# Sending every thirteenth load in two parts, partitions 0-119 and 120-127, in a two-layer decode step with its gradients

## The chip, the cores and the metric

The kernel runs on one core of one Trainium2 chip. The metric is the device time of one execution in microseconds (us); lower is better. Below, PE is TensorE, DVE is VectorE, ACT is ScalarE, POOL is GpSimd, SP is the engine from which most transfers are issued. "Line L257" is a line of the kernel before. MiB are 2^20 bytes, MB are 10^6.

## The reference: what is computed

Two identical blocks, attention against a long cache and a small MLP, are applied one after the other to a batch of two single tokens, and then the gradients of all inputs and weights are taken:

```python
def _A_ref(x, k_cache, v_cache, wq, wo):          # x 2x1x1024, caches 2x4x16384x128
    q = (x @ wq).reshape(B, Sq, 32, 128).transpose(0, 2, 1, 3)
    k = jnp.repeat(k_cache, 8, axis=1)
    v = jnp.repeat(v_cache, 8, axis=1)
    p = _softmax(jnp.einsum("bhqd,bhkd->bhqk", q, k) * 128 ** -0.5)
    o = jnp.einsum("bhqk,bhkd->bhqd", p, v)
    return o.transpose(0, 2, 1, 3).reshape(B, Sq, 4096) @ wo
def _B_ref(x, w1, b1, w2, b2):                    # w1 1024x3584, w2 3584x1024
    h = _gelu(_layernorm(x) @ w1 + b1)
    return h @ w2 + b2
for _ in range(2):
    x = x + _A_ref(_layernorm(x), k_cache, v_cache, wq, wo)
    x = x + _B_ref(_layernorm(x), w1, b1, w2, b2)
# outputs: x, and the gradients of x, k_cache, v_cache, wq, wo, w1, b1, w2, b2
```

All arrays are bf16. The two caches are 32 MiB each and are used by both layers, forward and backward, so they are read several times; their gradients, 32 MiB each, are most of what is written.

## The kernel before: tiles, queues and order of the work

The caches are cut into eight groups (batch times key head) of 128 partitions, and each group into four chunks of 32 rows a partition. A chunk is a tile of 128 partitions by 4096 bf16, 1 MiB, that is 8192 contiguous bytes for each partition. Weights come in tiles of the same size, or 896 KiB for w1: one row of 8192 or 7168 bytes a partition, or four rows of 2048 bytes.

All bulk loads are issued from SP's queue, in the order in which the program calls for them:

- `w_load` (L254, issue at L257) for the weights that pass through once (`w_pass`, L288, and the class `Ahead`, L343);
- `kv_load` (L404, issue at L409) for chunks of K and V in `attn_fwd` (L501) and `attn_bwd` (L593); a few chunks go to tiles that are kept (`keepK`, `keepV`, `keepxK`, `keepxV`);
- `load` in `wq_steps` (L877, issue at L886) for pieces of wq;
- `load_next` (L1198, issues at L1204 for wq and L1207 for K and V) in the last stage.

The loads share a pool `ld` of `NLD` = 7 buffers (L75, L81): SP's queue waits at a load until the last reader of the tile that was in the buffer is done. The work runs in stages: layer 0 forward and layer 1 forward (each a pass over wq, then K and V group by group, then wo and w1; w2 follows in layer 0), then layer 1 backward (w1, wo, V and K again, wq, w2), the MLP of layer 0 backward, and last the attention of layer 0 backward. `attn_fwd` turns each K chunk on TensorE (L420, copied out at L153 by ACT and L156 by DVE), takes scores (L573), exponentials (L537), and accumulates the V products (L452).

The last stage, from about 700 us, is where the outputs are made and stored. Its loop (L1434) turns a chunk of V (L1450), takes scores (L1312), and makes the gradients of K and V (`kv_pair`, L1247, matmuls at L1258) and of the weights (`dw_units`, L1162, matmuls at L1175). DVE (L164) and ACT (L161) cast the products into tiles, and `store` (L1137) sends these out. Stores go through POOL's software queue until L1480, where `pace["queue"]` becomes SP's queue for the last twelve. In this stage the pool's buffers are handed round by hand: `load_next` takes a tile whose store was issued or whose readers are done, so that a load may wait for a store to land. `pump` (L1209) issues loads ahead as far as free tiles allow. L1538 is the end of the program, where SP waits for the last stores.

Waits between engines are semaphores that the framework places from the program's reads and writes: a reader of a tile waits for every transfer that wrote it.

Of the kernel before, what the change touches and what calls it, by code (L numbers as in the profile page):

```python
# [2 lines left out]

# [20 lines left out]
def kernel(  # L24
# [24 lines left out]
    nc = tc.nc  # L49
# [4 lines left out]
    B, _, D = A_x.shape  # L54
# [11 lines left out]
    TC = 32  # L66
# [23 lines left out]
    ps_x = ctx.enter_context(tc.tile_pool(name="ps_x", bufs=4, space=PSUM))  # L90
    ps_acc = ctx.enter_context(tc.tile_pool(name="ps_acc", bufs=1, space=PSUM))
    ps_sm = ctx.enter_context(tc.tile_pool(name="ps_sm", bufs=1, space=PSUM))

    def pt(shape, dtype, name):
        return ps_tp.tile(shape, dtype, name=name, tag="tp")
# [74 lines left out]
    def wide_in(x2):  # L170

        return x2.unsqueeze(1).to_broadcast([128, WIDE // 2, 2])

    def wide_out(ps, c0):

        return ps[:, c0:c0 + WIDE].rearrange("p (a b) -> p a b", b=2)
# [77 lines left out]
    def w_load(W, j0, rb, n_cols):  # L254
        wt = ld.tile([128, LDW], BF16, name="wt", tag="ld")
        wv = wt[:, 0:rb * n_cols].rearrange("p (j n) -> p j n", j=rb)
        nc.sync.dma_start(wv, W[j0 * 128:(j0 + rb) * 128, :].rearrange("(j p) n -> p j n", p=128))  # L257
        return wv

    class BwdPipe:  # L260
# [57 lines left out]
    def turn(view, new_tp):  # L318

        tp = new_tp()  # L320
        for o in range(8):
            PE.transpose(tp[:, o, :], view[:, o * 128:(o + 1) * 128], ident[:])  # L322
        evac_bf16(view, tp[:].rearrange("p a b -> p (a b)"), 1024)
# [80 lines left out]
    def kv_load(w, g, c):  # L404
        keep = w + str(c) if g == G - 1 else w if (g, c) == (XG, 0) else None
        t = held_tiles[keep] if keep else ld.tile([128, LDW], BF16, name="kv_" + w, tag="ld")
        if keep not in held:
            src = Kv if w == "K" else Vv
            nc.sync.dma_start(t[:].rearrange("p (t d) -> p t d", d=128), src[g, :, c * TC:(c + 1) * TC, :])  # L409
            if keep:  # L410
                held.add(keep)
        return t[:].rearrange("p (t d) -> p t d", d=128)
# [12 lines left out]
    class Acc:  # L425
# [16 lines left out]
        def quad(self, c, q, coef=None):  # L442
            coef = coef or self.coef
            if q == 0 and self.get is not None:
                self.cv = self.get(c)
            elif q == 0:
                self.cv = self.pre.pop(c) if c in self.pre else kv_load(self.src, self.g, c)
            for i in range(8):
                u = c * CP + q * 8 + i
                cg = 32 * (i % 4)  # L450
                t = 2 * (q * 8 + i)
                PE.matmul(self.acc[cg:cg + 16, :], lhsT=coef(u),  # L452
                          rhs=self.cv[:, t:t + 2, :].rearrange("p t d -> p (t d)"),
                          start=False, stop=True, tile_position=(0, cg), skip_group_check=True)
# [46 lines left out]
    def attn_fwd(l, q_bf, rbc, oT, groups):  # L501
# [79 lines left out]
        while s < len(slots) + 2 or sch.busy():  # L581
            sch.s = s
            if s < len(slots):
                g, c, b = slots[s]
                if b == 0:
                    cv = kv_load("K", g, c)
                kTs[s] = emit_T(cv, b, True)
            sch.run_slot(1 if s < len(slots) else 2)
            if 2 <= s < len(slots) + 2:
                score(s - 2)  # L590
            s += 1

    def attn_bwd(l, do_bf, dqT, dn, groups, ahead):  # L593
# [40 lines left out]
        def post(g, c):  # L634
# [21 lines left out]
            if g == groups[-1]:  # L656
                accs[g].pre[c] = kv_load("K", g, c)
                if c == NCH - 1:
                    for k in range(NLD - 2):
                        ahead.load(k)  # L660
                        j0, rb = ahead.chunks[k]
                        w2_q.extend(lambda j=j: ahead.row(j) for j in range(j0, j0 + rb))
# [212 lines left out]
    wq_v = A_wq.rearrange("(j p) n -> p j n", p=128)  # L875

    def wq_steps(l, kv, dqT, dn, new_tp, new_ps, get_=None, done_=lambda *job: None):  # L877

        hs = slice(kv * 8, kv * 8 + 8)
        box = {}  # L880

        def load(j):
            wt = ld.tile([128, LDW], BF16, name="wqt", tag="ld") if get_ is None else get_("wq", kv, j)
            box[j] = wt[:].rearrange("p (j n) -> p j n", j=4)
            if get_ is None:
                nc.sync.dma_start(box[j], wq_v[:, j:j + 4, kv * D:(kv + 1) * D])  # L886

        def turn_row(j):
            turn(box[j - j % 4][:, j % 4, :], new_tp)

        def products(j0=0):
            ps = new_ps()
            for j in range(j0, DJ):
                for o in range(8):
                    PE.matmul(wide_out(ps, 2 * j), lhsT=box[j - j % 4][:, j % 4, o * 128:(o + 1) * 128],
                              rhs=wide_in(dq_all[:, kv * 8 + o, 2 * l:2 * l + 2]), start=(o == 0), stop=(o == 7))
            V.tensor_tensor(out=dn[:, j0:DJ], in0=dn[:, j0:DJ],
                            in1=ps[:, 2 * j0:2 * DJ].rearrange("p (j b) -> p j b", b=2), op=ALU.add)
            for j in (0, 4):
                done_("wq", kv, j)  # L900

        def dq_in():
            for b in range(2):
                V.tensor_copy(out=dq_all[:, hs, 2 * l + b], in_=dqT[:, b * HKV + kv, :])

        return [lambda j=j: load(j) for j in (0, 4)], dq_in, [lambda j=j: turn_row(j) for j in range(DJ)], products, box
# [31 lines left out]
    for k in range(NLD - 2, len(w2b.chunks)):  # L938
        w2b.load(k)
        j0, rb = w2b.chunks[k]  # L940
# [193 lines left out]
    def load_tile():  # L1134
        return (by_read or by_store if opening["on"] else by_store or by_read).popleft()

    def store(out_ap, view, tile_):  # L1137
        pace["queue"].dma_start(out_ap, view)
        if tile_ is not None:
            by_store.append(tile_)  # L1140

# [10 lines left out]
    def dbias(rows, i, n, out_ap, name):  # L1152
        p = 32 * i
        row = new_home()
        for c0 in range(0, n, 512):
            ps = mx()
            PE.matmul(ps[p:p + 1, :], lhsT=ones_bf[p:p + 4, 0:1], rhs=rows[p:p + 4, c0:c0 + 512], start=True, stop=True,
                      tile_position=(p, p))
            evac_cast(row[p:p + 1, c0:c0 + 512], ps[p:p + 1, :], 512)
        store(out_ap.rearrange("(o f) -> o f", o=1), row[p:p + 1, 0:n], row)  # L1160
# [37 lines left out]
    def load_next():  # L1198
        job = jobs.popleft()
        t = loaded[job] = load_tile()  # L1200
        open_loads.append(job)
        if job[0] == "wq":
            src = wq_v[:, job[2]:job[2] + 4, job[1] * D:(job[1] + 1) * D]
            nc.sync.dma_start(t[:].rearrange("p (j n) -> p j n", j=4), src)  # L1204
        else:
            src = (Kv if job[0] == "K" else Vv)[job[1], :, job[2] * TC:(job[2] + 1) * TC, :]
            nc.sync.dma_start(t[:].rearrange("p (t d) -> p t d", d=128), src)  # L1207

    def pump(most, spare):  # L1209
        while jobs and len(open_loads) < most and n_free() > spare:  # L1210
            load_next()

    def get(*job):
        while job not in loaded:
            load_next()
        return loaded[job]
# [30 lines left out]
    def kv_pair(w, i, h):  # L1247

        g, c = chunks[i]
        if h == 0:  # L1250
            stgs[w, i] = new_home()
        sv_ = stgs[w, i][:].rearrange("p (b r t d) -> p b r t d", r=4, t=2, d=128)
        blk, Qm = blks[w, i], qms[w, g]
        o = 0 if w == "V" else NB
        pss = [mx() for _ in range(4)]
        for b in range(2):
            for r in range(4):
                PE.matmul(pss[r][:, b * 256:(b + 1) * 256], lhsT=blk[32 * r:32 * r + 32, o + 2 * h + b, :],  # L1258
                          rhs=Qm[32 * r:32 * r + 32, :, :].rearrange("p a b -> p (a b)"), start=True, stop=True,
                          tile_position=(32 * r, 0))  # L1260
        for r in range(4):
            evac_cast(sv_[:, 2 * h:2 * h + 2, r], pss[r][:].rearrange("p (b t d) -> p b t d", b=2, t=2), 512)
        if h == 0:
            split[w, i] = pace["short"] or i >= NC - 2
        if h == 1 or split[w, i]:
            lo = h if split[w, i] else 0
            dst = (dVv if w == "V" else dKv)[g, :, c * TC + lo * TC // 2:c * TC + (h + 1) * TC // 2, :]
            store(dst, stgs[w, i][:, lo * LDW // 2:(h + 1) * LDW // 2].rearrange("p (t d) -> p t d", d=128),
                  stgs[w, i] if h == 1 else None)
# [214 lines left out]
    i, g = NC - 1, order[-1]  # L1484
    kv = g % HKV
# [57 lines left out]
```

## Time and profile before

| what | value |
|---|---|
| median of 3 runs | 1139.71 us (1137.65 to 1144.74) |
| the profiled execution, its own time | 1138.65 us |
| its span in the profile | 1136.9 us, 40053 instructions |
| busy: PE, PEld (weight loads), DVE, ACT, POOL | 944.5, 730.9, 633.7, 564.7, 70.9 us |
| mean granted TensorE clock | 0.857 of full speed |
| moved by DMA | 449.31 MB in 91983 packets, mean 395 GB/s |
| read from and written to the main memory | 348.14 MB and 98.58 MB |
| K and V loads to `ld` tiles before the last stage | 81 each, 1 MiB, 11.8 and 12.2 us from issue to landing |

The page of the profile gives busy times of the engines and, in 40 equal slices of the span (28.4 us each), the mean busy share of the core's sixteen DMA engines in tenths and the GB/s that they moved. Queue q1 is SP's, q0 is POOL's software queue, q8 and q14 fetch instructions. A row of the windows view gives, for a stretch of time, each engine's busy us with its number of instructions, then the granted TensorE clock, the DMA engines' share and GB/s. A row of the waits view reads: who waited, at which line, for what; us in total, times, the longest. A DMA share can come out a little above 1, since packets of one engine overlap by about 3 ns.

### The profile page before, as it was taken

What the parts mean: (1) busy time and instruction counts of PE and PEld (TensorE: products, weight loads), DVE (VectorE), ACT (ScalarE), POOL (GpSimd) and SP (SyncE); (2) the same over time, 40 slices, a digit from 0 to 9 for tenths busy, and PEclk for the clock granted to TensorE, in tenths of its full rate; (3) what the DMA queues carried; (4) which work ended last, traced back from release to release, by engine and by line L of the source; (5) the groups of instructions that cost most, each with busy time, mean ns of one, the idle gap of its engine ahead of it and who ended that gap; (6) DMA issues with size and microseconds to landing.
All of it is one profiled execution on the core that took longest, in us unless ns stands there. A gap on an engine that the chain in (4) does not pass through costs nothing.

```text
span 1136.9 us, 40053 instructions
## 1 busy us (share of the span) xinstructions
PE 944.5 (83%) x17566; PEld 730.9 (64%) x17567; DVE 633.7 (56%) x1356; ACT 564.7 (50%) x1415; POOL 70.9 (6%) x126
## 2 busy tenths in 40 slices
PE   4989895487879885899988689989898989999884
PEld 3867674487767665888876578855555555555551
DVE  1545451133545432554846454678877868786784
ACT  0535351022535340343554344667777767786673
POOL 0000000000000000000000000022111112111210
PEclk9989796596999876899998799998987868896895
DMA  8999999998999989999999999998999999999996
GB/s 370 424 425 423 425 424 413 409 378 354 424 425 423 425 310 413 408 369 411 367 422 418 351 359 355 346 378 318 376 421 423 421 419 421 421 422 420 423 423 256
DMA packets 91983, 449.31 MB, mean 395 GB/s; under 512 B 7318, under 2 KB 7318, under 8 KB 54688
## 3 DMA queue, kind: packets, MB, share of 16 engines
q1 hardware_dynamic: 74448, 354.46, 77.4%
q0 software_dynamic: 17360, 92.29, 19.7%
q8 instruction: 137, 2.24, 0.7%
q14 instruction: 38, 0.31, 0.1%
HBM read 348.14 MB, written 98.58 MB: 393 GB/s over the span
## 4 chain that ended last, share of the span: by engine, by line
PE 55%; DMA 23%; DVE 11%; ACT 6%; issue 4%; POOL 0%; DVEq 0%; ACTq 0%; POOLq 0%
DMA kv_V<-in_A_v_cache_dram 13%; PE tp L420 10%; PE tpm L1450 5%; PE wtp L270 5%; PE acc_all L452 4%; PE xm L1258 4%; PE xm L1175 3%; DMA wt<-in_A_wo_dram 3%; PE sc L573 3%; DMA kv_K<-in_A_k_cache_dram 3%; PE dp L1312 3%; PE turn L322 3%; DMA keepK<-in_A_v_cache_dram 2%; PE dp L672 2%; DVE big L164 2%
## 5 line engine op out<-in xcount | busy, mean ns | idle before, releaser
L153 ACT COPY kT<-tp 128x512 int32<-128x512 int32 x209 | 122.6, 586 | 253.6 <-PE tp L420 242.5
L156 DVE COPY kT<-tp 128x1024 bf16<-128x1024 bf16 x159 | 108.6, 691 | 110.0 <-PE tp L420 97.8
L420 PE MATMUL tp<-ident,kv_K 128*128 128x128 bf16 x1728 | 145.5, 234 | 4.3 <-DMA kv_K<-in_A_k_cache_dram 4.2
L420 PEld LDWEIGHTS <-kv_K 128*128 128x128 bf16 x1728 | 110.2, 104 | 5.1 <-DMA kv_K<-in_A_k_cache_dram 4.8
L164 DVE CAST big<-xm 128x512 bf16<-128x512 f32 (+1 forms) x125 | 81.2, 686 | 24.6 <-PE xm L1258 16.8
L573 PEld LDWEIGHTS <-kT 128*128 128x128 bf16 x2048 | 76.6, 98 | 28.1 <-issue 21.9
L573 PE MATMUL sc<-qT_bf,kT 128*128 128x8 bf16 x2048 | 92.2, 172 | 0.9 <-issue 0.7
L161 ACT CAST big<-xm 128x512 bf16<-128x512 f32 (+1 forms) x139 | 75.6, 593 | 25.2 <-PE xm L1258 16.2
L420 PE MATMUL tp<-ident,kv_V 128*128 128x128 bf16 x864 | 70.8, 229 | 10.7 <-DMA kv_V<-in_A_v_cache_dram 9.0
L270 PE MATMUL wtp<-ident,wt 128*128 128x128 bf16 x928 | 74.8, 227 | 3.4 <-issue 2.2
L537 ACT ACTIVATE e_all<-sc,negm 128x64 bf16<-128x64 f32 x256 | 77.0, 344 | 1.3 <-DVE negm L532 1.2
L306 PEld LDWEIGHTS <-wt 128*128 128x128 bf16 x1696 | 48.9, 103 | 44.3 <-issue 14.9
L161 ACT CAST keepV<-xm 128x512 bf16<-128x512 f32 x116 | 63.5, 595 | 24.1 <-PE xm L1258 18.4
L452 PE MATMUL acc_all<-kv_V,e_all 128*16 128x256 bf16 x864 | 45.6, 291 | 25.5 <-DVE acc_all L435 12.3
L156 DVE COPY wT<-wtp 128x1024 bf16<-128x1024 bf16 (+1 forms) x64 | 40.7, 641 | 46.6 <-PE wtp L270 43.0
L153 ACT COPY wT<-wtp 128x512 int32<-128x512 int32 (+1 forms) x60 | 34.2, 571 | 62.5 <-PE wtp L270 48.2
L164 DVE CAST keepV<-xm 128x512 bf16<-128x512 f32 x88 | 56.9, 685 | 14.1 <-PE xm L1258 9.5
L164 DVE CAST keepK<-xm 128x512 bf16<-128x512 f32 (+1 forms) x86 | 55.8, 685 | 16.1 <-PE xm L1258 10.8
L420 PEld LDWEIGHTS <-kv_V 128*128 128x128 bf16 x864 | 55.8, 102 | 11.7 <-DMA kv_V<-in_A_v_cache_dram 9.7
L161 ACT CAST keepK<-xm 128x512 bf16<-128x512 f32 (+1 forms) x96 | 52.0, 592 | 16.7 <-PE xm L1258 15.2
L537 ACT ACTIVATION_READ_ACCUMULATOR e_all<-sc,negm 128x1 f32 x256 | 60.2, 236 | 0.0
L270 PEld LDWEIGHTS <-wt 128*128 128x128 bf16 x928 | 57.2, 101 | 4.1 <-issue 2.7
(366 smaller groups left out, 1785.0 us busy)
## 6 DMA issues: line engine op xcount, KB each, us to landing
kv_K<-in_A_k_cache_dram SPq DMA_DIRECT2D x81, 1024.0 KB, 11.8
kv_V<-in_A_v_cache_dram SPq DMA_DIRECT2D x81, 1024.0 KB, 12.2
wt<-in_A_wo_dram SPq DMA_DIRECT2D x32, 1024.0 KB, 10.3
wt<-in_B_w_dram SPq DMA_DIRECT2D x32, 896.0 KB, 14.1
out_dram<-big POOLq DMA_DIRECT2D x25, 1024.0 KB, 16.8
out_dram<-keepK POOLq DMA_DIRECT2D x18, 1024.0 KB, 19.8
wt<-in_A_wq_dram SPq DMA_DIRECT2D x16, 1024.0 KB, 9.0
wt<-in_B_w_dram SPq DMA_DIRECT2D x14, 1024.0 KB, 12.9
```

The source lines that it names most:

```text
L153: S.copy(out=dst.bitcast(I32), in_=src.bitcast(I32))
L156: V.tensor_copy(out=dst, in_=src)
L161: S.copy(out=dst, in_=src)
L164: V.tensor_copy(out=dst, in_=src)
L270: PE.transpose(tp[:, o, :], wv[:, j, (o0 + o) * 128:(o0 + o + 1) * 128], ident[:])
L306: PE.matmul(fps[:, jo, :].rearrange("p (a b) -> p a b", b=2), lhsT=wv[:, j, jo * 128:(jo + 1) * 128], rhs=xT_bf[:, j0 + j, :].unsqueeze(1) ...
L420: PE.transpose(tp[:, j, :], cv[:, b * 8 + j, :], ident[:])
L452: PE.matmul(self.acc[cg:cg + 16, :], lhsT=coef(u), rhs=self.cv[:, t:t + 2, :].rearrange("p t d -> p (t d)"), start=False, stop=True, tile_ ...
L537: S.activation(out=e_all[:, g, f * half:(f + 1) * half, l, h, :], in_=sc[g][f][:, h, :].rearrange("p (a b) -> p a b", b=2), func=ACT.Exp, ...
L573: PE.matmul(sc[g][f][:, :, t % TH], lhsT=kT[:, j, :], rhs=q_bf[:, g, :], start=True, stop=True)
L1258: PE.matmul(pss[r][:, b * 256:(b + 1) * 256], lhsT=blk[32 * r:32 * r + 32, o + 2 * h + b, :], rhs=Qm[32 * r:32 * r + 32, :, :].rearrange(" ...
L1450: PE.transpose(tp[:, j, :], cv[:, b * 8 + j, :], ident[:])
```

## The change

A function `load_` takes the place of the direct issue at five lines (L257, L409, L886, L1204, L1207). It adds up the MiB of every load and every store; whenever 13.3 MiB have gone by since the last time, the load at hand goes out as two transfers from SP's queue, one of partitions 0 to 119 and one of partitions 120 to 127, into the same tile. The count starts at 6. `store` counts what it sends, and is otherwise as before; the rows of x, grad_out and the biases (`load_row`) and the two small result rows are neither split nor counted. Nothing else changes: order, tiles, buffers and arithmetic are the same.

```diff
+    moved = {"mb": 6.0}
+
+    def count_dma(mb):
+        moved["mb"] += mb
+
+    def load_(dst, src):
+
+        count_dma(math.prod(dst.shape) * 2 / 2.0 ** 20)
+        if moved["mb"] < 13.3:
+            nc.sync.dma_start(dst, src)
+            return
+        moved["mb"] -= 13.3
+        nc.sync.dma_start(dst[0:120], src[0:120])
+        nc.sync.dma_start(dst[120:128], src[120:128])
+
...
-        nc.sync.dma_start(wv, W[j0 * 128:(j0 + rb) * 128, :].rearrange("(j p) n -> p j n", p=128))
+        load_(wv, W[j0 * 128:(j0 + rb) * 128, :].rearrange("(j p) n -> p j n", p=128))
...
-            nc.sync.dma_start(t[:].rearrange("p (t d) -> p t d", d=128), src[g, :, c * TC:(c + 1) * TC, :])
+            load_(t[:].rearrange("p (t d) -> p t d", d=128), src[g, :, c * TC:(c + 1) * TC, :])
...
-                nc.sync.dma_start(box[j], wq_v[:, j:j + 4, kv * D:(kv + 1) * D])
+                load_(box[j], wq_v[:, j:j + 4, kv * D:(kv + 1) * D])
...
         pace["queue"].dma_start(out_ap, view)
+        count_dma(math.prod(view.shape) * 2 / 2.0 ** 20)
...
-            nc.sync.dma_start(t[:].rearrange("p (j n) -> p j n", j=4), src)
+            load_(t[:].rearrange("p (j n) -> p j n", j=4), src)
...
-            nc.sync.dma_start(t[:].rearrange("p (t d) -> p t d", d=128), src)
+            load_(t[:].rearrange("p (t d) -> p t d", d=128), src)
```

More of the change, by code (lines that the diff above doesn't have):

```diff
@@ L1 @@
+import math
 from collections import deque
```

## Prediction, on record before the result

> **What bounds the kernel now.** I read the page's parts 2 and 3 first (is the traffic the limit, and whose), then the busy time by windows, then who waited for whom, and last the tail. Part 2 and part 3 of the page:
>
> ```profile
> DMA  8999999998999989999999999998999999999996
> GB/s 370 424 425 423 425 424 413 409 378 354 424 425 423 425 310 413 408 369 411 367 422 418 351 359 355 346 378 318 376 421 423 421 419 421 421 422 420 423 423 256
> ...
> q1 hardware_dynamic: 74448, 354.46, 77.4%
> q0 software_dynamic: 17360, 92.29, 19.7%
> q8 instruction: 137, 2.24, 0.7%
> ```
>
> The sixteen DMA engines are nearly always busy, and 425 GB/s is their ceiling here: in the trace's packets one of 8192 B lasts 309 ns and the next on its engine starts 306 ns after it, which is 26.8 GB/s an engine, 428 for sixteen. Loads (q1) are most of it; stores (q0) begin at about 700 us. By windows:
>
> ```profile
> core 0: us, PE busy (x) PEld busy (x) DVE busy (x) ACT busy (x) POOL busy (x), PEclk, DMA share, GB/s
> 300.00:350.00 50.00, 42.08 (x841) 34.32 (x840) 23.70 (x54) 23.24 (x106) 0.00 (x0) 0.93 1.01 425
> ...
> 550.00:600.00 50.00, 45.02 (x985) 36.29 (x984) 32.60 (x74) 27.04 (x49) 0.00 (x0) 1.00 0.98 396
> ...
> 1050.00:1100.00 50.00, 42.46 (x660) 27.82 (x652) 39.74 (x70) 37.07 (x71) 9.92 (x14) 0.93 1.02 423
> ```
>
> TensorE and the DMA engines are both close to full: in the attention stages and in the last 250 us the DMA share is 1, while between them compute sets the pace. What TensorE waits for tells the two kinds of DMA-full stage apart. Up to 700 us, and then from 850 us:
>
> ```profile
> PE acc_all L452 <- DMA kv_V<-in_A_v_cache_dram: 11.9, 12, 1.8
> PE acc_all L306 <- DMA wt<-in_A_wo_dram: 10.3, 8, 1.6
> PE tp L420 <- DMA kv_V<-in_A_v_cache_dram: 9.0, 5, 3.8
> ```
>
> ```profile
> PE tpm L1450 <- DMA keepK<-in_A_v_cache_dram: 2.1, 1, 2.1
> ```
>
> So the early stages do wait for loads, many times, and the late one hardly: there DVE and ACT are 0.8 and 0.75 busy too, and SP's long waits for stores (L1207) are hidden. The tail is different:
>
> ```profile
> 1128.00:1130.00 2.00, 0.00 (x0) 0.00 (x0) 0.00 (x0) 0.00 (x0) 0.00 (x0) 0.91 0.93 359
> 1130.10:1135.10 5.00, 0.00 (x0) 0.00 (x0) 0.00 (x0) 0.00 (x0) 0.00 (x0) 0.50 0.06 25
> ```
>
> ```profile
> SPq L1538 <- DMA out_dram<-big: 7.4, 1, 7.4
> ```
>
> Nothing computes after 1127.6, and from 1130.1 to 1135.1 the DMA share is 0.06 = 1/16 at 25 GB/s: **one** engine works off a backlog while fifteen are done. The kernel's end waits for it (L1538).
>
> I also read the sixteen landings that each transfer posts in the trace's semaphore updates. In the pure load stage, 300 to 375 us, engines split into two groups: eight keep the nominal pace, the other eight fall 1.4 us behind one after another, each once in some 66 us, every time an instruction packet (137 of 16384 B, 935 ns, and a stretched packet behind it) passes. By 371 us those eight lie within 0.43 us of each other, so **no single engine is slow while only loads run** (under 0.6% in 75 us). In the store stage one landing is apart from the fifteen others: 4.4 us behind the next at 1001 us, 5.9 to 11.4 at 1050 to 1092, 5.1 at the last transfer.
>
> [...]a laggard appears only with q0 traffic; its number is not in the trace.[...]
>
> **The change part by part.** *How often.* 449.31 MB less 2.55 of instructions is 426 MiB; with the starting 6 and less the 10 MiB of stores issued after the last load (1085 us), 422/13.3 gives 31 splits. Part 2's first 25 slices sum to 282 MB = 269 MiB by 710 us, so (269+6)/13.3 = 20 fall there, one per 33 us, and 11 later; from 850 to 1085 us, at 421 GB/s, 7.
> [...]
> *Tail.* If the laggard is engine 15 the last transfer ends with the fifteen: 1135.2 − 1130.0 = **−5.2 us**. What is late next is the chain of casts and SP's store issues up to 1127.7, which the change does not touch. [...]from 1110 to 1125 us the share is 0.93, then 0.46, about 3.4 us free.
> *Store stage.* Loads and freed buffers come a few us earlier; all that waits is the 2.1 us above. I take **−1** (between 0 and −2).
> *Load stages.* [...]in the 300 us with share 1.01 or more and no stores (50 to 250, 300 to 400) that is 9 x 0.31 = 2.8.[...] All 20 splits: 6.2. I take **+1.5**.
> *SP.* 31 more issues at 0.33 us (a kv_V load's issue) = 10 us. SP stands idle for hundreds of us before loads (L409 alone 148 us for L452); the second part is 0.33 us late behind the first, and only the next load is queued behind it. 0; without cover 0.33 us a split.
> *Waits.* A reader now waits for two semaphores. The trace shows no price for it; at most one issue gap (L1175, 36.3/121 = 0.3 us), 9 us for 31, at least nothing. In DMA-bound stages TensorE waits for the later one anyway: 0.
> [...]between nothing and half rate for the first part, 2.45 us a split[...]. I take 0, since the engines are out of step by up to 4.5 us at 400 us, but keep the other end.
>
> *Sum.* Span 1136.9 − 5.2 − 1 + 1.5 = 1132.2; around it lies 1138.65 − 1136.9 = 1.75, so 1134.0 against the profiled 1138.65. The median of the runs is 1.06 above that one: **1135**.
>
> **The rivals.**
> *A, the tail goes (0.58):* 1135, own range 1131 to 1139. For it: the one-sixteenth share after 1130.
> *B, the laggard is another engine, or the split leaves another out (0.17):* the change then does not do what it says; tail stays, cost stays: 1139.7 + 1.5 = 1141, up to 1146 with all 6.2. For it: no engine numbers in the trace, and no laggard in the load stage.
> *C, slower[...] (0.17):* the 120-partition part runs at half rate in the load stages. 9 splits x 2.45 = 22: 1139.7 − 5.2 + 22 = 1157[...]. It beats the tail's gain from 5.2/9 = 0.58 us a split on, and is worth over 1% from (11.4 + 5.2)/9 = 1.84. Against it: engines out of step overlap only in part, and compute hides some.
> *D, faster (0.08):* the laggard paces the stores and by L1207 the loads and compute behind them; stage 850 to 1110 shrinks from 421 to 428 GB/s, 1.6% of 260 = 4.3 us, and with the whole wait and tail, and some for the middle stages at 700 to 850, 12 to 14 us: 1126.
>
> **How the numbers follow.** The time is A's. Range 1129 to 1152: it holds A, B, and C's milder half, leaving out D and C at full price. About 1% (11.4 us) is what a measurement of this kernel can tell from no change (its three runs spread over 7 us). Faster by over 1% (below 1128.3): D and A's edge, 0.10. Slower (above 1151.1): most of C, 0.14. Within: 0.76.
>
> **What would show it.** Right: after the last cast no stretch with a share of 0.06; L1538's wait falls from 7.4 to about 2; 31 loads of 960 KB and 31 of 64 KB; the last store's sixteen landings within a us. Wrong: the one-engine stretch is still there (B); 8192-B packets well over 309 ns, or DMA waits of TensorE before 700 us that grow by over 10 us (C); SP's L1207 waits falling with the whole store stage shorter (D).

## The result, and the profile after

The changed kernel takes 1244.35 us (median of 4 runs, 1231.97 to 1251.49) against 1139.33 us (4 runs, 1137.65 to 1144.74). Its runs fall in two groups, 1232 to 1238 and 1251; the ratio, 1.083 (1.075 to 1.091), is made of the shorter ones, about +95 us, and the profiled execution (1251.49 us, span 1249.7) is of the longer kind. The forecast was 1135 us, in a range that ended at 1152.

Parts 2 and 3 of the page of the kernel after, the same rows as shown of before:

```profile
DMA  9999999998999997999999999999999999999996
GB/s 323 390 401 352 335 341 369 380 304 277 385 407 325 337 354 268 371 365 356 365 372 356 341 299 331 336 322 363 321 396 389 416 417 404 401 413 403 417 420 259
...
q1 hardware_dynamic: 74665, 354.46, 78.4%
q0 software_dynamic: 17360, 92.29, 18.3%
q8 instruction: 137, 2.24, 0.7%
```

Read the two rows together. The DMA engines are as busy as ever, but in the first 29 slices they move 268 to 407 GB/s where before they moved up to 425. They are not waiting for work; the same work takes longer. The bytes of q1 are unchanged, and its packets are 217 more: 31 splits, each with 15 + 8 completion packets instead of 16, make 31 x 7 = 217. So there are 31 splits, and fifteen engines work for the part of 120 partitions and eight for the part of 8: in the trace's semaphore updates the one posts 15 landings and the other 8, where a whole load posts 16. One engine is left out; which one is not in the trace. The change does what it says.

The windows of the kernel after (columns as before):

```profile
50.00:100.00 50.00, 41.84 (x770) 34.09 (x766) 22.00 (x47) 23.03 (x112) 0.00 (x0) 0.80 1.01 359
...
350.00:400.00 50.00, 39.12 (x706) 31.37 (x704) 19.81 (x44) 18.26 (x79) 0.00 (x0) 0.81 1.01 367
550.00:600.00 50.00, 44.66 (x961) 41.52 (x962) 24.34 (x58) 19.76 (x34) 0.00 (x0) 0.94 1.01 373
1000.00:1050.00 50.00, 44.11 (x567) 26.58 (x565) 36.56 (x66) 33.82 (x66) 6.87 (x12) 0.80 1.02 417
```

And two of the same windows in the kernel before:

```profile
50.00:100.00 50.00, 43.57 (x852) 35.44 (x849) 23.41 (x51) 21.03 (x95) 0.00 (x0) 0.86 1.01 424
1000.00:1050.00 50.00, 45.18 (x579) 26.59 (x578) 38.06 (x69) 35.33 (x67) 7.35 (x12) 0.80 1.02 421
```

In the load stages the share is 1.01 at 359 to 373 GB/s, where before it was 1.01 at 424; from 550 to 600 us too, where before the share was 0.98 at 396. In the last stage 417 GB/s are left of 421. The loss is in the load stages: taken matmul by matmul, TensorE is some 7 us behind the kernel before at 56 us of that kernel's time, 52 behind at 317, 101 at 705, and 113 at 1121.

What TensorE waits for in the whole run, first in the kernel before (three lines that the prediction does not show), then in the kernel after (L468 is L452 of before, L436 is L420, L322 is L306):

```profile
PE acc_all L306 <- DMA wt<-in_A_wq_dram: 8.0, 5, 2.7
PE acc_all L306 <- DMA wt<-in_B_w_dram: 7.4, 6, 1.3
PE tp L420 <- DMA kv_K<-in_A_k_cache_dram: 4.2, 6, 1.4
```

```profile
PE acc_all L468 <- DMA kv_V<-in_A_v_cache_dram: 29.6, 18, 3.8
PE tp L436 <- DMA kv_K<-in_A_k_cache_dram: 21.2, 11, 4.0
PE acc_all L322 <- DMA wt<-in_B_w_dram: 18.6, 9, 4.1
PE acc_all L322 <- DMA wt<-in_A_wq_dram: 14.4, 7, 4.4
PE acc_all L322 <- DMA wt<-in_A_wo_dram: 12.9, 8, 2.9
PE tp L436 <- DMA kv_V<-in_A_v_cache_dram: 11.7, 7, 4.2
```

All six waits shown are longer in total than before: kv_V at the V products went from 11.9 to 29.6 us, kv_K from 4.2 to 21.2, the weights w from 7.4 to 18.6. On these three tiles the longest single wait is now about 4 us, where it was 1.3 to 1.8; 4 us is about what one split turns out to cost.

The tail, by windows and by SP's waits at the end of the program (L1555):

```profile
1242.00:1245.00 3.00, 0.00 (x0) 0.00 (x0) 0.00 (x0) 0.00 (x0) 0.00 (x0) 0.59 0.44 168
1245.00:1249.50 4.50, 0.00 (x0) 0.00 (x0) 0.00 (x0) 0.00 (x0) 0.00 (x0) 0.50 0.05 20
```

```profile
SPq L1555 <- DMA out_dram<-keepV: 2.4, 2, 1.2
SPq L1555 <- DMA out_dram<-big: 2.4, 2, 1.2
SPq L1555 <- DMA out_dram<-keepK: 2.3, 2, 1.2
```

The stretch with one engine at work is still there, and SP now waits for six stores one after another, 1.2 us each: that is one engine's share of such a store, eight packets of 4096 B at 159 ns or sixteen of 2048 B at 84 ns. In the last store one landing comes 5.3 us after fourteen others.

Further readings of the trace's packets. The mean packet of 8192 B on q1 takes 355 ns instead of 319, and 4157 of 30976 take over 1.3 times the median instead of 730; only 31 x 120 = 3720 belong to first parts of split loads, fewer where the rows are shorter. After each split the engines together move about half as much for 8 to 10 us (180 to 260 GB/s instead of 425, behind six of the splits between 50 and 380 us), and in the six us in which they move least, 82% of the 8192-byte packets take over 450 ns (ten splits between 20 and 420 us), so it is not one or two engines that are held up. Summed over packets, an engine is busy 92 us longer than before in the stages up to the last (20 splits, 4.6 us each) and 12 us longer in the last (11 splits, 1.1 each).

### The profile page after: what moved, and what is told of

Read it like the earlier page. It is cut to its first block, busy times and chain, and to the rows that moved or that the text cites. A ratio compares the mean times of both kernels' runs of the same rounds, so it can differ in the third digit from the quotient of the medians.

```text
span 1249.7 us, 40120 instructions
## 1 busy us (share of the span) xinstructions
PE 979.6 (78%) x17566; PEld 754.5 (60%) x17567; DVE 633.6 (51%) x1356; ACT 566.6 (45%) x1415; POOL 71.1 (6%) x126
## 4 chain that ended last, share of the span: by engine, by line
PE 42%; DMA 41%; DVE 10%; issue 4%; ACT 3%; POOL 0%; DVEq 0%; SPq 0%; POOLq 0%; ACTq 0%
DMA kv_V<-in_A_v_cache_dram 18%; PE tp L436 8%; DMA out_dram<-keepK 6%; PE wtp L286 5%; DMA kv_K<-in_A_k_cache_dram 4%; PE acc_all L468 4%; DMA wt<-in_A_wo_dram 3%; PE tpm L1467 3%; PE sc L589 3%; PE xm L1275 2%; PE turn L338 2%; DMA wt<-in_B_w_dram 2%; DMA out_dram<-keepV 2%; DMA keepV<-in_A_k_cache_dram 2%; PE xm L1192 2%
## 5 line engine op out<-in xcount | busy, mean ns | idle before, releaser
L436 PE MATMUL tp<-ident,kv_K 128*128 128x128 bf16 x1728 | 152.3, 241 | 21.3 <-DMA kv_K<-in_A_k_cache_dram 21.2
L436 PEld LDWEIGHTS <-kv_K 128*128 128x128 bf16 x1728 | 115.7, 108 | 22.5 <-DMA kv_K<-in_A_k_cache_dram 22.4
L322 PEld LDWEIGHTS <-wt 128*128 128x128 bf16 x1696 | 49.1, 104 | 61.6 <-DMA wt<-in_B_w_dram 19.5
L436 PE MATMUL tp<-ident,kv_V 128*128 128x128 bf16 x864 | 73.1, 233 | 15.3 <-DMA kv_V<-in_A_v_cache_dram 11.7
L468 PE MATMUL acc_all<-kv_V,e_all 128*16 128x256 bf16 x864 | 50.3, 317 | 41.6 <-DMA kv_V<-in_A_v_cache_dram 29.6
L436 PEld LDWEIGHTS <-kv_V 128*128 128x128 bf16 x864 | 57.7, 105 | 17.5 <-DMA kv_V<-in_A_v_cache_dram 12.7
```

Of the source, the lines that this page charges most:

```text
L322: PE.matmul(fps[:, jo, :].rearrange("p (a b) -> p a b", b=2), lhsT=wv[:, j, jo * 128:(jo + 1) * 128], rhs=xT_bf[:, j0 + j, :].unsqueeze(1) ...
L436: PE.transpose(tp[:, j, :], cv[:, b * 8 + j, :], ident[:])
L468: PE.matmul(self.acc[cg:cg + 16, :], lhsT=coef(u), rhs=self.cv[:, t:t + 2, :].rearrange("p t d -> p (t d)"), start=False, stop=True, tile_ ...
```

## The experiments

Each kernel is the changed one with another `load_`, unless a diff says otherwise, and each was compared with the kernel before on the same chip.

**Does it take an engine left out?** Two parts of 64. With 64 partitions all sixteen engines can be at work: in the table below the even part of `evenodd`, 64 packets of 309 ns, takes 1.2 us, about sixteen at a time. In the first of the halves, 64 packets of 640 ns in 2.7 us are 15.2 at a time; by the same estimate the change's first part, with its fifteen engines, has 13.4 (120 of 601 ns in 5.4 us).

```diff
-        nc.sync.dma_start(dst[0:120], src[0:120])
-        nc.sync.dma_start(dst[120:128], src[120:128])
+        nc.sync.dma_start(dst[0:64], src[0:64])
+        nc.sync.dma_start(dst[64:128], src[64:128])
```

> The same 31 loads go out in two parts, but of partitions 0-63 and 64-127: each part runs on all sixteen engines[...].[...] each part takes 8 x 0.306 = 2.45 us instead of 1.22, so 2.45 us a split, 31 splits, +76 us: 1215 us (1195 to 1230). Fewer than sixteen engines are what costs (rival): sixteen are used here, so no change, 1139 us. Two transfers for one load are what costs, with a second semaphore and a second issue (rival): as the changed kernel, 1244 us.

1233.69 us, ratio 1.082 (1.076 to 1.088): as slow as the change. Windows of that run:

```profile
50.00:100.00 50.00, 39.09 (x744) 31.83 (x741) 21.71 (x45) 22.89 (x112) 0.00 (x0) 0.83 1.02 360
```

The same 360 GB/s. So the loss does not need an engine left out; that two transfers go out for one load is still open here.

**Two transfers as such.** All 128 partitions, half the columns each: two issues, two semaphores, all partitions in both transfers.

```diff
-        nc.sync.dma_start(dst[0:120], src[0:120])
-        nc.sync.dma_start(dst[120:128], src[120:128])
+        for h in range(2):
+            if d1 > 1:
+                s = slice(h * d1 // 2, (h + 1) * d1 // 2)
+                nc.sync.dma_start(dst[:, s, :], src[:, s, :])
...
```

> The same 31 loads go out in two parts, but each of all 128 partitions with half of the columns: two transfers, two semaphores and two issues, sixteen engines[...].[...] no loss but for sixteen half rows at 6 ns more an engine, 0.05 us a split: 1139 to 1142 us. Fewer engines: 1139 us. Two transfers: 1244 us.

1140.27 us, ratio 1.000 (0.998 to 1.002). Windows:

```profile
50.00:100.00 50.00, 43.30 (x838) 35.18 (x836) 23.31 (x50) 21.25 (x96) 0.00 (x0) 0.86 1.01 423
300.00:350.00 50.00, 41.46 (x832) 33.99 (x829) 23.51 (x53) 22.74 (x100) 0.00 (x0) 0.93 1.01 425
```

SP's second issue, the second semaphore and the second set of completions cost nothing that can be seen.

**Another bound,** 112 in place of 120.

```diff
+        nc.sync.dma_start(dst[0:112], src[0:112])
+        nc.sync.dma_start(dst[112:128], src[112:128])
```

> The same 31 loads in parts of partitions 0-111 and 112-127: nearly the cut of the changed kernel[...].[...] 1.0 us a split if the engines run in step, up to 2.8 if they lag[...]: +31 to +87 us, 1170 to 1226 us. Fewer engines: 1139 us. Two transfers: 1244 us.

1215.99 us, ratio 1.066 (1.060 to 1.072): +75 us, 2.4 a split. The first part covers 112 partitions, not 64; most of the loss stays. How many engines work for it was not shown.

**Which splits cost?** `early` splits only the 20 loads before the last stage, `late` only the 11 in it (a flag set at that stage's start).

```diff
-        if moved["mb"] < 13.3:
+        if moved["mb"] < 13.3 or moved["late"]:          # early
...
+        if not moved["late"]:                            # late
+            nc.sync.dma_start(dst, src)
+            return
```

> Loads are split as in the changed kernel, but only before the last stage (some 20 of the 31 splits). By the trace of the changed kernel these loads carry 92 of its 103 us of stretched packets an engine,[...] 1240 us (1225 to 1250).[...] If every split counted alike: 20/31 of 105, +68 us, 1207 us.

> Loads are split as in the changed kernel, but only in the last stage (11 of the 31), where stores share the engines and compute hides much. From the trace of the changed kernel, 12 us of stretched packets an engine: +13 us, 1153 us (1145 to 1160). If every split counted alike: 11/31 of 105, +37 us, 1177 us.[...]

`early`: 1229.72 us, ratio 1.075 (1.066 to 1.084), +86. `late`: 1153.46 us, ratio 1.009 (1.006 to 1.013), +10. The two add up to the change's +95. The GB/s row of `early`, and then that of `late`:

```profile
GB/s 320 398 395 355 336 350 380 336 317 306 416 379 352 353 359 354 371 349 354 383 359 371 364 316 343 310 348 379 328 379 400 420 423 420 424 422 421 422 421 287
```

```profile
GB/s 372 424 425 423 425 425 412 404 365 371 424 424 418 423 310 424 389 369 415 373 419 419 343 367 330 359 310 312 386 389 418 417 421 413 399 415 406 395 420 235
```

Each kernel has the slow rows only where it splits; in `late` they are 395 to 421 and not 320 to 400. The late landing at the end is there in `late` too, 5.6 to 6.2 us behind. Summed over packets as above, an engine is busy 85 us longer in `early` before the last stage, and 11 us longer in `late` in it.

**The dose.** 15 splits.

```diff
-        if moved["mb"] < 13.3:
+        if moved["mb"] < 26.6:
...
-        moved["mb"] -= 13.3
+        moved["mb"] -= 26.6
```

> The changed kernel with a split at every 26.6 MiB instead of 13.3, about half as many (15 or 16). Each split pays for itself and is over within some 10 us[...]: half of the loss, +50 us, 1190 us (1180 to 1200). If a split instead left the engines out of step for good, so that the loss does not depend on their number: over three quarters of it, above 1218 us.

1182.02 us, ratio 1.033 (1.026 to 1.040), +38: somewhat under half. A split costs by itself; one does not put the engines out of step for good.

**Which engine is late at the end?** No load is split; the last store goes out in parts of ever fewer partitions. A part that lands whole does not use the late engine. (The second run has the same edit with other sizes.)

```diff
...
+            for n in (60, 28, 12, 10, 8, 6, 4):
+                pace["queue"].dma_start(out_ap[a:a + n], view[a:a + n])
+                a += n
```

> No load is split. The very last store goes out from the same queue in seven parts of 60, 28, 12, 10, 8, 6 and 4 partitions[...]. The landings of each part tell whether the engine that ends 5 us after the others is in that set.[...] one landing of every part whose set holds it comes about 5 us late. Time as before, 1139 us, within 3.

> No load is split. The last store goes out in parts of 60, 28, 20, 6, 5, 5 and 4 partitions[...].[...] the parts of five still have a landing 2.5 us or more behind their others, and the part of four has none.[...] If another engine is late in each execution, the border lies elsewhere. Time: 1140 to 1147 us either way.

`tail_sets`, 1146.09 us: the parts of 60, 28, 12, 10, 8 and 6 partitions each have one landing 2.7 to 3.7 us behind the others, and the part of four, issued last, lands whole and before all of these. `tail_sets2`, 1140.01 us: both parts of five partitions have one landing 2.8 and 3.4 us behind, the part of four has none. So the late engine works for the part of 60 partitions and for small ones as well, down to six in the one execution and five in the other, and not for the part of four. The trace gives no numbers of engines, so which one it is was not shown.

**Does the software queue make it late?** No load is split. The stores of the last stage, but for the twelve that SP's queue issues, go out from ACT's queue (`act_stores`), or only those that are issued after the last load go out from SP's (`sync_tail`).

```diff
-    opening, pace = {"on": True}, {"short": True, "queue": nc.gpsimd}
+    opening, pace = {"on": True}, {"short": True, "queue": nc.scalar}
```

```diff
-        pace["queue"].dma_start(out_ap, view)
+        (nc.sync if not jobs and not opening["on"] else pace["queue"]).dma_start(out_ap, view)
```

> The kernel before, no load split, but the stores of the last stage are issued from the ACT engine instead of the software queue. If the one engine that ends 5 us late is late because of the software queue, the stretch with a sixteenth of the DMA share at the end goes: -5 us, if ACT's issues (some 78 at 0.3 us, 25 us of its time in the last stage, and its waits for DVE's casts) cost nothing, 1135 us; with them up to 1165. If the laggard comes from elsewhere, the stretch stays, and the time is 1140 or more.

> No load is split. Once all loads are issued, the stores that still went through the software queue go through SP's hardware queue (the last four of them, issued at 1090 to 1101 us in the kernel before). If the late engine gathers its lag from every transfer of the software queue, and these four are what is left to work off at the end: 3 to 5 us less than before, the one-engine stretch at the end under 2 us. If the lag was there by 1090 us already (11 us), and is only worked off: no change in the time, within 2 us, and a landing still 4 us or more behind the others.

`act_stores` is slower, 1173.26 us, ratio 1.026 (1.020 to 1.031), more than the 1165 that was allowed for (why was not looked into), but its tail is clean; windows of that run:

```profile
1165.00:1170.00 5.00, 2.49 (x8) 0.66 (x5) 2.60 (x4) 2.40 (x5) 0.00 (x0) 0.84 0.94 369
1170.00:1173.00 3.00, 0.00 (x0) 0.00 (x0) 0.00 (x0) 0.00 (x0) 0.00 (x0) 0.50 0.23 87
```

The sixteen landings of each of the last stores lie within 0.3 us. `sync_tail`: 1141.49 us, ratio 0.999 (0.997 to 1.001). Its last landings are still 3.4 to 4.0 us late. The last five stores of its software queue have a landing 10 to 12 us behind the others, the last of them at 1126 us, while the four stores moved to SP's queue have no such landing (the last within 0.7 us of the one before it). So the lag belongs to the software queue's stores and is gathered before the last load. No version that beats the kernel before came of it.

**Where a part writes.** A part of even and one of odd partitions have the size and the number of transfers of the halves.

```diff
+        nc.sync.dma_start(dst[0:128:2], src[0:128:2])
+        nc.sync.dma_start(dst[1:128:2], src[1:128:2])
```

> The same 31 loads go out in two transfers of 64 partitions each, as in the halves run, but the even and the odd partitions instead of the lower and the upper.[...] no loss, 1140 us, within 5 us of the kernel before. Rival, that any transfer of fewer than 128 partitions costs what the halves cost: about 1233 us. A rival between them, that two parts in flight at once disturb each other: anything from 1160 to 1200.

1142.04 us, ratio 1.001 (0.999 to 1.003). Windows:

```profile
50.00:100.00 50.00, 41.93 (x818) 33.96 (x816) 22.79 (x50) 20.22 (x90) 0.00 (x0) 0.87 1.01 424
300.00:350.00 50.00, 42.10 (x803) 34.20 (x800) 21.86 (x50) 22.13 (x98) 0.00 (x0) 0.86 1.01 425
```

Nothing is lost. The halves and these parts differ on both sides, in the rows that they read and the partitions that they write. Two kernels exchange one side each, `low_from_even` and then `even_from_low`:

```diff
+        nc.sync.dma_start(dst[0:64], src[0:128:2])
+        nc.sync.dma_start(dst[64:128], src[1:128:2])
```

```diff
+        nc.sync.dma_start(dst[0:128:2], src[0:64])
+        nc.sync.dma_start(dst[1:128:2], src[64:128])
```

> Of the 31 split loads, the first part writes partitions 0 to 63 from the even rows of the source, the second partitions 64 to 127 from the odd rows, so the rows of these tiles are exchanged among one another, which changes the values and not the amount of work. If the loss of the halves comes from where they write in the on-chip memory: 1233 us as the halves, from 1220 to 1245. If it comes from how they read the main memory: 1141 us as the even and odd parts.

> The other pairing: of the 31 split loads, the first part writes the even partitions from rows 0 to 63 of the source, the second the odd partitions from rows 64 to 127; again only rows of these tiles are exchanged. If the loss comes from where the parts write: 1141 us. If it comes from how they read: 1233 us. A value between in both runs would say that both sides count.

`low_from_even`: 1228.99 us, ratio 1.075 (1.070 to 1.081). `even_from_low`: 1141.11 us, ratio 1.001 (0.999 to 1.002). Windows of the one, then of the other:

```profile
50.00:100.00 50.00, 38.46 (x735) 31.92 (x732) 21.49 (x45) 22.40 (x109) 0.00 (x0) 0.86 1.01 363
```

```profile
50.00:100.00 50.00, 43.55 (x851) 35.40 (x849) 23.54 (x51) 20.94 (x94) 0.00 (x0) 0.86 1.01 424
```

Which rows are read makes no difference. **The loss goes with the partitions that are written.**

**Within one half.** Four parts of 32, in steps of two, each within one half of the partitions.

```diff
+        for a in (0, 1, 64, 65):
+            nc.sync.dma_start(dst[a:(a | 63) + 1:2], src[a:(a | 63) + 1:2])
```

> The 31 loads go out in four parts of 32 partitions: even and odd ones of partitions 0 to 63, then even and odd ones of 64 to 127.[...] as the halves did: 1215 to 1235 us. If what counts is only that an engine's share is a run of consecutive partitions (no two of a share are neighbours here): 1141 us, with at most 10 us for the 93 more transfers.

1223.51 us, ratio 1.073 (1.069 to 1.077). The step of two does not help once a part stays in one half. That cannot be all of it: the parts of partitions 0 to 111 and 0 to 119 do not stay in one half, and those kernels lose as well (1.066 and 1.083).

**Which of the two parts?** The first part in even and odd partitions, the second as it was.

```diff
+        for a in (0, 1):
+            nc.sync.dma_start(dst[a:120:2], src[a:120:2])
+        nc.sync.dma_start(dst[120:128], src[120:128])
```

> The change with its first part, partitions 0 to 119, sent as the even and then the odd ones of them[...]; the second part, 120 to 127, as in the change. If a run of neighbouring partitions in an engine's share is what costs, only the second part's loss is left:[...] 1140 to 1170. If the eight partitions of the second part carry the loss by themselves: 1235 to 1250 as the change.

> The same with the bound at 112: even and odd ones of partitions 0 to 111[...], then partitions 112 to 127[...]. If the run of neighbours costs: 1140 to 1170. If the last sixteen partitions carry the loss: 1216 as the run with 0 to 111 and 112 to 127.

1228.26 us, ratio 1.073 (1.069 to 1.077), and 1227.84 us, ratio 1.072 (1.068 to 1.077). Time alone would put the loss on the second part, but the landings and packets say otherwise. From the trace, in ten splits of 1 MiB loads between 20 and 420 us (eleven for even and odd): the time from the median landing of one transfer (the middle one of those that its engines post) to the median landing of the next, for the first parts and then for the whole way from the load before the split to the second load behind it (medians, us). Nominal is 0.306 us for each row of the engine that has most of them when the rows of a part are spread as evenly as they can be over sixteen engines. The last column is the median length of an 8192-byte packet that starts after the median landing of the load before and ends before any engine is done with the first part (ns).

```text
kernel         first part(s), nominal            up to two loads later, nominal   packet
change         5.4 (2.45)                        12.0 (7.7)                       601
p112           4.3 (2.14)                        11.5 (7.3)                       554
halves         2.7 (1.22)                        11.7 (7.3)                       640
four_parts     1.2, 1.3, 1.1, 1.1 (0.61 each)    11.1 (7.3)                       533
step_112       3.0, 2.2 (1.22 each)              11.8 (7.7)                       515
step_120       2.6, 2.4 (1.22 each)              11.7 (7.7)                       536
even and odd   1.2, 1.2 (1.22 each)               7.7 (7.3)                       309
```

Taking it that each engine works off SP's transfers in their order, none of the fifteen engines with a share in the change's first part has begun the second when the first landing of the first part comes. So **the first part alone runs at half speed**: its packets take 601 ns where a whole load's take 309 (`early`, with the same splits, gives 5.5, 12.1 and 609). The same goes for the even and odd parts in `step_120`: about half speed with 60 partitions each (536 ns), while even and odd parts of 64 run at full speed (309 ns). (In `step_112`, 515 ns, engines without a share in the first two parts, if there are any, may be at the third already.) All kernels that lose, lose about the same by the second load behind, 3.8 to 4.4 us a split, whatever the shape of the parts; in the halves a third of that falls on the whole load right behind them, which takes 3.9 us instead of 2.45. The edit therefore did not take the first part's cause away, as its expectation had supposed; a run of neighbours is not what is needed for the loss. What the second part costs by itself was not tried: no kernel had a first part free of loss.

## Why the prediction was wrong

*How often* was right: 31 splits, 20 of them before the last stage.

***The price of a slower first part* is the step that failed.** Its far end, half rate and 2.45 us a split, was the author's estimate, which no trace of the kernel before showed. It took 0, "since the engines are out of step by up to 4.5 us at 400 us". They are out of step, and it does not help: a split in the load stages costs about 4.3 us in the mean (`early`: 86/20; the landings give 12.0 − 7.7 = 4.3). The packets show the disturbance spread over 8 to 10 us rather than avoided. The idea behind rival C, a first part at half rate, was right (601 ns a packet against 309); its price, 2.45 us a split against the 4.3 measured, was too low.

**C's count was the second error.** It took 9 splits, those in windows with a share of 1.01 and no stores, and so ended at 1157. `early` is worth all 20 at a full price: 20 x 2.45 = 49 would have given about 1184 with the tail's gain. The windows that it left out had shares like 0.98, so there was little idle DMA time to take up 4 us; that share was in the prediction's own fence.

*Tail* failed by its premise: "if the laggard is engine 15" it is −5.2. Engine 15 is the author's name there for the engine that the part of 120 partitions leaves out. By the author's estimate it has 8 rows less (128/16), 8 x 0.306 = 2.45 us a split and 17 us in 7 splits of the store stage, more than the 11.4 us that the laggard is ever behind; but that the laggard is this engine was not shown. Where it was looked for, in two executions without splits, the laggard works for a part of 60 partitions and for parts of six and of five. In the changed kernel the stretch stays. Rival B had this right, and its own price (+1.5 to +6) was lost in the larger loss. The laggard's link to the software queue is borne out by `act_stores`, where the landings of each of the last stores lie within 0.3 us.

*Store stage* and *load stages* were small terms for a tail and for the second part's row, 0.31 us on each of eight engines; `late` gives +10 for the 11 splits there instead of −1. A split costs 0.9 us there and not 4.3, and not because the rest is hidden: the packets themselves are stretched less (1.1 us an engine and split). Why was not tried; over half of that stage's bytes are stores (98.6 of 171 MB in the kernel before).

*SP* and *Waits* at 0 were right: `columns` makes as many issues and waits at ratio 1.000.

Shown, then: after a split the packets take about twice as long (515 to 640 ns instead of 309), and whether they do depends on the partitions that the parts write, not on there being two transfers (`columns`, `evenodd`), and for parts of 64 not on the source rows (`even_from_low`, `low_from_even`). An engine left out is not needed for it (`halves`, with 15.2 packets at a time in the first part against 13.4 in the change's). But the number of engines may matter: even and odd parts are free with 64 partitions each (`evenodd`, ratio 1.001, about sixteen packets at a time), and at about half speed with 60 or 56, and no run tells the number of engines from the partitions there. That the cause of the 120-partition part lies on the writing side is carried over from the halves, not tried. Not shown is the path to it: the trace tells neither an engine's number nor the rows that it moves. Rows dealt in order, equally many to each engine, would not explain it by themselves: the first fifteen engines would then write the same even partitions in `evenodd` and in `step_120`, and only the first kernel is free.

## What to carry to other kernels

Where loads set the pace, don't split a 128-partition load into runs of partitions: 31 splits of 1 MiB or less cost 7 to 8% here, and nothing when the same loads were cut by columns or into the even and the odd ones of all 128 partitions. Before a split is costed at nothing because engines are out of step, look at the GB/s next to the DMA share: a share of 1 at fewer GB/s (here 1.01 at 359 instead of 424) means that packets take longer, and here the whole loads behind a split were slowed with it. An edit that aims at one DMA engine needs to know which: a transfer cut into parts of ever fewer partitions shows in one or two runs for which of them the late engine works (here for six and for five, and not for four).

## What the runs showed of the hardware

- A load sent as 0 to 119 and 120 to 127, as 0 to 111 and 112 to 127, or as two halves holds up the others for long: a whole load of 1 MiB takes 2.45 us, and after such a split the engines run at about half speed for 8 to 10 us, and 3.8 to 4.4 us a split are lost by the second load behind.
- Even and odd partitions of all 128 are as good as a whole load (`evenodd`: 7.7 us for three loads' rows, 7.4 in the kernel before); even and odd ones of 0 to 119 take 2.4 to 2.6 us each (`step_120`), where the even and odd ones of all 128 take 1.2.
- One engine lags where the stores go through the software queue, by up to 11.4 us (the kernel before) and 13.1 us (the kernel after) in that queue's own stores; the last landing of the last whole store is 0.6 us (`columns`) to 5.6 us (`late`) behind the one before it. With ACT's queue it is 0.03 us, but that kernel is 30 us slower.
